# An attention and gated-MLP kernel: V tiles set once, copies placed by an estimate of two queues, 15 packed score batches, one x block loaded by itself

## Chip, cores, metric

The kernel runs on one core of one Trainium2 chip. The metric is device time in microseconds (us), lower is better. The granted clock is the share of TensorE's full clock that the trace records. Engines are named as in the profile: PE is TensorE, PEld its weight loads, DVE is VectorE, ACT is ScalarE, POOL is GpSimd, SP issues most DMAs.

## The reference

One transformer block on x of 2048 x 512, bf16. After a layer norm, two branches are added to x: attention with 32 heads of 16, causal with a window of 256 keys, and a gated linear MLP of width 1792.

```python
def _A_ref(x, wqkv, wo):                       # H = 32, Dh = 16, W = 256
    q, k, v = ...                              # of x @ wqkv
    scores = jnp.einsum("bhqd,bhkd->bhqk", q, k) * (Dh ** -0.5)
    mask = (idx[:, None] - idx[None, :] >= 0) & (idx[:, None] - idx[None, :] < W)
    p = _softmax(jnp.where(mask[None, None], scores, -1e9), axis=-1)
    return ...einsum("bhqk,bhkd->bhqd", p, v)... @ wo
def _B_ref(x, w_gate, w_up, w_down):
    h = (x @ w_gate) * (x @ w_up)
    return h @ w_down
xn = _layernorm(x)
return x + _A_ref(xn, ...) + _B_ref(xn, ...)
```

## The kernel before

The 2048 rows go in four chunks T of 512. PE's stream is laid out by hand: every few dense 512-column matmuls (gate, up, down, projections: the "fillers") a batch of small score matmuls is put in. ScalarE takes the exp of each batch, VectorE masks its diagonal, GpSimd masks its far edge with up to 4 affine selects. The row sums of the softmax come from columns of ones that stand in the V tile beside the values.

```python
# tiles: four PSUM banks "M" for dense results, the two value sums included;
# four banks for the one score tile S
self.ps_m = pool("ps_m", 4, space=bass.MemoryType.PSUM)
# ... setup
for lo, hi in ((0, 1), (1, 4)):                # x block 0, then blocks 1 to 3
    nc.sync.dma_start(out=self.x[:, lo:hi, :], in_=xv[:, lo:hi, :])
for _ in range(38):                            # warm-up
    nc.tensor.matmul(wps[:], lhsT=ident[:], rhs=ident[:], start=True, stop=True)
# ...
def new_chunk(self, T):                        # a filler of no cost, once a chunk
    self.V[T] = self.chunk3.tile([128, VW], BF16, tag="V", name=f"V{T}")
    # ... Q, K, Ko, VS
    nc.gpsimd.memset(self.heads(self.V[T])[:, :, :, 16:18], 1.0)
    nc.gpsimd.memset(self.V[T][:, VW - 16:], 0.0)
    nc.gpsimd.memset(self.VS[T][:, SW - 16:], 0.0)
def proj_v(self, t, ks=range(4)):              # ... four matmuls into a bank M, then
    nc.scalar.activation(out=self.heads(self.V[T])[:, b]..., in_=ps..., func=ACT.Copy)
def gate(self, T, f, ks):                      # likewise for K and Q
    if self.act_free:                          # 11 units or more after the last batch
        nc.scalar.activation(out=self.gsb[:], in_=ps[:], func=ACT.Copy)
    else:
        nc.vector.tensor_copy(out=self.gsb[:], in_=ps[:])
# first chunk: for b in 0..3: normalize block b on VectorE, statistics of block b + 2;
# then transposes and V projections of the four blocks, then K and Q
```

The softmax here doesn't subtract the row's maximum and nothing guards it: scores larger than these inputs give would overflow.

Of the kernel before, what the change touches and what calls it, by code (L numbers as in the profile page):

```python
# [18 lines left out]
FIRST = (((5, 5, 7), (0, 0, 4)), ((3, 3, 5), (1, 1, 5)),  # L19
         ((3, 6, 7), (7, 7, 7), (2, 2, 6)), ((4, 4, 7), (6, 6, 7)))  # L20
LATER = (((-2, 0, 2), (0, 0, 4)), ((5, 5, 7), (1, 1, 5)), ((-3, 0, 1), (7, 7, 7), (3, 3, 7)),
         ((-4, 0, 0), (6, 6, 7), (2, 2, 6)), ((-1, 0, 3), (4, 4, 7)))
ACT_FREE = 11


class Kernel:
# [26 lines left out]
    def setup(self):  # L53
# [11 lines left out]
        for lo, hi in ((0, 1), (1, 4)):  # L65
            nc.sync.dma_start(out=self.x[:, lo:hi, :], in_=xv[:, lo:hi, :])
# [41 lines left out]
        self.strips, self.at = {}, {}  # L108

    def new_chunk(self, T):  # L110

        self.Q[T] = self.chunk2.tile([128, 4, 512], BF16, tag="Q", name=f"Q{T}")
        self.K[T] = self.chunk3.tile([128, 4, 512], BF16, tag="K", name=f"K{T}")
        self.Ko[T] = self.chunk3.tile([128, 4, 512], BF16, tag="Ko", name=f"Ko{T}")
        self.V[T] = self.chunk3.tile([128, VW], BF16, tag="V", name=f"V{T}")
        self.VS[T] = self.chunk3.tile([128, SW], BF16, tag="VS", name=f"VS{T}")
        nc = self.nc
        nc.gpsimd.memset(self.heads(self.V[T])[:, :, :, 16:18], 1.0)
        nc.gpsimd.memset(self.V[T][:, VW - 16:], 0.0)
        nc.gpsimd.memset(self.VS[T][:, SW - 16:], 0.0)  # L120
# [21 lines left out]
    def norm_stats(self, t, n=4):  # L142

        nc = self.nc
        if t % n == 0:
            self.mv = self.small.tile([128, n, 2], F32, tag="mv", name="mv")
        st = self.small.tile([128, 6], F32, tag="st")
        nc.vector.bn_stats(out=st[:], in_=self.x[:, t, :])  # L148
        nc.vector.bn_aggr(out=self.mv[:, t % n, :], in_=st[:])
        self.stats[t] = [self.mv, t % n, None]  # L150
# [13 lines left out]
    def norm_apply(self, t):  # L164
        nc = self.nc
        mv, j, rs = self.stats.pop(t)
        xn = self.xpool.tile([128, 512], BF16, tag="xn", name="xn")
        nc.vector.tensor_scalar(out=xn[:], in0=self.x[:, t, :], scalar1=mv[:, j, 0:1],  # L168
                                scalar2=rs[:, j:j + 1], op0=ALU.subtract, op1=ALU.mult)
        self.xns[t] = xn  # L170
# [24 lines left out]
    def proj_v(self, t, ks=range(4)):  # L195
        nc = self.nc
        T, b = divmod(t, 4)
        ps = self.bank(ks, "vp")
        for k in ks:
            nc.tensor.matmul(ps[:], lhsT=self.xnT[T][:, b, k, :],  # L200
                             rhs=self.Wqkv[:, k, 1024:1536], start=(k == 0), stop=(k == 3))
        if 3 not in ks:
            return
        nc.scalar.activation(out=self.heads(self.V[T])[:, b].rearrange("p (r g) d -> p r g d", r=2)[:, :, :, 0:16],
                             in_=ps.rearrange("p (g r d) -> p r g d", g=16, r=2), func=ACT.Copy)

    def proj_qk(self, T, c, is_k, ks=range(4), on_act=False):
        nc = self.nc
        lo = 512 * is_k + 128 * c
        ps = self.bank(ks, "qkp")  # L210
        for k in ks:
            nc.tensor.matmul(ps[:], lhsT=self.Wqkv[:, k, lo:lo + 128], rhs=self.xnT[T][:, :, k, :],  # L212
                             start=(k == 0), stop=(k == 3))
        if 3 not in ks:
            return
        if is_k:
            if self.act_free:
                nc.scalar.activation(out=self.K[T][:, c, :], in_=ps[:], func=ACT.Copy)
            else:
                nc.vector.tensor_copy(out=self.K[T][:, c, :], in_=ps[:])  # L220
            nc.vector.tensor_scalar(out=self.Ko[T][:, c, :], in0=self.K[T][:, c, :],
                                    scalar1=self.odd[:, 0:1], scalar2=None, op0=ALU.mult)
        elif on_act or self.act_free:
            nc.scalar.activation(out=self.Q[T][:, c, :], in_=ps[:], func=ACT.Copy)
        else:
            nc.vector.tensor_copy(out=self.Q[T][:, c, :], in_=ps[:])

    def first_chunk(self):

        self.new_chunk(0)  # L230
        for b in range(2):
            self.norm_stats(b, 1)
            self.norm_scale(b, 1)
        for b in (0, 1, 2, 3):
            self.norm_apply(b)
            if b < 2:
                self.norm_stats(b + 2, 1)
                self.norm_scale(b + 2, 1)
        self.norm_transpose(0, False)
        for b in range(4):  # L240
            if b < 3:
                self.norm_transpose(b + 1, False)
            self.proj_v(b)
        self.proj_qk(0, 0, 1)
        self.proj_qk(0, 0, 0, on_act=True)
        self.swap_halves(0, self.nc.scalar)
        self.proj_qk(0, 1, 1)


    def scores(self, T, c, pieces):  # L250

        nc = self.nc
        S = self.s_tiles.tile([128, 4, 512], F32, tag="S", name="S")
        col = 0
        for m, q0, q1 in pieces:
            U, j = divmod(8 * T + m, 8)
            keys, q, n = slice(64 * j, 64 * j + 64), 64 * q0, 64 * (q1 - q0 + 1)
            for par in range(2):
                for e in range(4):
                    rows = slice(32 * e, 32 * e + 16 + 16 * par)  # L260
                    nc.tensor.matmul(S[64 * par:64 * par + 64, e, col:col + n],  # L261
                                     lhsT=(self.Ko if par else self.K)[U][rows, c, keys],
                                     rhs=self.Q[T][rows, c, q:q + n],
                                     start=True, stop=True, tile_position=(32 * e, 64 * par),
                                     skip_group_check=True)
            col += n
        P = self.ppool.tile([128, 4, 512], BF16, tag="P", name="P")
        nc.scalar.activation(out=P[:, :, 0:col], in_=S[:, :, 0:col], func=ACT.Exp, scale=0.25)  # L268
        self.strips[(T, c, pieces)] = P
# [4 lines left out]
    def places(self, pieces, far):  # L274

        out, at = [], 0
        for m, q0, q1 in pieces:
            out += [at + 64 * (q - q0) for q in range(q0, q1 + 1) if q == m + far]
            at += 64 * (q1 - q0 + 1)
        return out  # L280

    def mask_diag(self, T, c, pieces):

        P = self.strips[(T, c, pieces)]
        places = [at // 64 for at in self.places(pieces, 0)]
        step = places[1] - places[0] if len(places) == 2 else 1
        v = P.rearrange("p e (b x) -> p e b x", x=64)[:, :, places[0]:places[-1] + 1:step, :]
        n = len(places)
        self.nc.vector.tensor_tensor(out=v, in0=v, op=ALU.min,  # L289
                                     in1=self.diag.unsqueeze(1).unsqueeze(1).to_broadcast([128, 4, n, 64]))  # L290

    def values(self, T, c, accs=None):
# [5 lines left out]
        todo = []  # L298
        for pieces in LATER if T else FIRST:
            P, col = self.strips.pop((T, c, pieces)), 0  # L300
            for m, q0, q1 in pieces:
                todo.append((P, col, m, 64 * q0, 64 * (q1 - q0 + 1)))
                col += 64 * (q1 - q0 + 1)
# [17 lines left out]
        for par in range(2):  # L321
            nc.vector.transpose(out=at[:, par].rearrange("p b r -> p (b r)"), in_=accs[par][:])  # L322
        self.at[(T, c)] = at

    def divide(self, T, c):
# [5 lines left out]
        if c == 0:  # L331
# [3 lines left out]
                                in1=rz.unsqueeze(3).to_broadcast([128, 2, 16, 16]), op=ALU.mult)  # L335
        nc.vector.transpose(out=self.OT[T][:, c, :], in_=on.rearrange("p b r d -> p (b r d)"))


    def gate(self, T, f, ks):
# [10 lines left out]
        if self.act_free:  # L350
            nc.scalar.activation(out=self.gsb[:], in_=ps[:], func=ACT.Copy)  # L351
        else:
            nc.vector.tensor_copy(out=self.gsb[:], in_=ps[:])  # L353

    def up(self, T, f, ks):
# [7 lines left out]
        nc.vector.tensor_tensor(out=self.hT[T][:, f, :], in0=ps[:], in1=self.gsb[:], op=ALU.mult)  # L363

# [28 lines left out]
    def store(self, T, b, part=0, on_act=False):  # L393
# [7 lines left out]
        else:  # L401
            nc.vector.tensor_tensor(out=y, in0=ps, in1=self.x[:, t, c0:c1], op=ALU.add)
        (nc.scalar if on_act else nc.sync).dma_start(out=self.out_d[128 * t:128 * t + 128, c0:c1], in_=y)


    def fillers(self):
# [73 lines left out]
        for b in range(4):  # L480
# [3 lines left out]
            if b in (1, 3):  # L484
                add(1, lambda b=b: self.add_x(T, b, 0 if b == 1 else 1))
        return [(*o, None, None)[:4] for o in out]

    def run(self):
        self.xns, self.stats, self.sums = {}, {}, {}
        self.act_free = False  # L490
# [5 lines left out]
        for T in range(NCH):  # L496
            for c in range(4):
                self.first[T, c] = len(steps)
                for pieces in LATER if T else FIRST:
                    self.last[T, c] = len(steps)  # L500
                    steps.append((T, c, pieces))
        due = {g: key for key, g in self.last.items()}
        SCORES, VALUES = 1.85, 5.5
# [3 lines left out]
        spent, n, scored = 0, 0, 0  # L507
        valued, ready = -1, -1

        def fill(upto, group):  # L510
            nonlocal spent, n
            while n < len(work):
# [6 lines left out]
                self.act_free = spent + cost - scored >= ACT_FREE  # L519
                f()  # L520
                spent += cost
                n += 1

        def values(g):
            nonlocal spent
            if g not in due:
                return False
            self.values(*due[g])
            spent += VALUES
# [7 lines left out]
        for g, s in enumerate(steps):  # L537
            fill(-1, g)
            valued = ready
            self.scores(*s)  # L540
            scored = spent
            spent += SCORES
# [21 lines left out]
        for b in range(3):  # L564
            self.wo(T, b, (3,))
            self.store(T, b, on_act=(b == 1))
# [42 lines left out]
```

## Time and profile before

| | before |
|---|---|
| median of 3 runs | 269.21 us (269.17 to 269.22) |
| profiled span | 267.5 us |
| PE, DVE, ACT, POOL busy | 97%, 68%, 64%, 43% |

From the page of the kernel before: the span, the busy times of part 1, and part 4, the chain of work that ended last, followed back from the end and summed by engine and by line.

```profile
span 267.5 us, 8861 instructions
...
PE 258.4 (97%) x3860; PEld 119.1 (45%) x3882; DVE 181.7 (68%) x352; ACT 170.6 (64%) x132; POOL 113.8 (43%) x281
...
PE 88%; DVE 7%; issue 1%; DMA 1%; ACT 1%; SPq 0%; POOL 0%; DVEq 0%; POOLq 0%
PE up L359 17%; PE gp L345 17%; PE psd L378 16%; PE qkp L212 11%; PE S L261 9%; PE acc L316 6%; PE psd L384 5%; PE vp L200 4%; PE L L378 2%; DMA x<-in_A_x_dram 1%; DVE hT L363 1%; DVE st L148 1%; DVE at L322 1%; DVE gsb L353 1%; DVE xn L168 1%
```

PE carries the chain. The 7% of DVE in it are about 19 us, of which some 13 lie in one stretch that comes below.

The opening, from the timeline of the kernel before (columns: start us, duration us, engine, line, operation, out<-in, shapes, count, and in brackets the engine's idle time before it and what ended it):

```profile
4.80 0.70 DVE L148 BATCH_NORM_STATS2 st<-x 128x6 f32<-128x512 bf16 x1 [0.84 <-DMA x<-in_A_x_dram]
...
5.63 0.38 DVE L168 TENSOR_SCALAR xn<-x,mv,rs 128x512 bf16<-128x512 bf16 x1
...
9.14 0.41 DVE L168 TENSOR_SCALAR xn<-x,mv,rs 128x512 bf16<-128x512 bf16 x1 [0.77 <-POOL rs L160]
...
11.74 0.59 PE L212 MATMUL qkp<-xnT,Wqkv 128*128 128x512 bf16 x2
```

The statistics of block 1 wait for the load of blocks 1 to 3. Everything to the last normalize at 9.14 follows from that, and the dense stream of PE (first qkp matmul at 11.74) from the last normalize.

A place that I read too quickly, from the same timeline, with DVE's rows left in:

```profile
36.51 0.68 DVE L353 CAST gsb<-gp 128x512 bf16<-128x512 f32 x1
36.56 0.60 PE L359 MATMUL up<-xnT,Wu 128*128 128x512 bf16 x2
...
37.24 1.02 PE L345 MATMUL gp<-xnT,Wg 128*128 128x512 bf16 x4
...
42.47 0.69 DVE L363 TENSOR_TENSOR hT<-up,gsb 128x512 bf16<-128x512 f32 x1
...
42.89 0.26 PE L316 MATMUL acc<-P,VS 64*32 64x192 bf16 x4
...
43.22 0.33 PE L316 MATMUL acc<-P,V 64*32 64x192 bf16 x8
```

Two up matmuls start at 36.56 and 226 ns later, so the gate matmul should start 216 ns after that, at 37.01 (six qkp matmuls from 11.74 take 1.46 us, the last of them drawn 0.38 long: 1.08 / 5 = 0.216). It starts at 37.24, just after VectorE's gate copy ends at 37.19, which by the program frees the bank that it read. The value matmuls likewise break off until VectorE's product ends at 43.16: this group of 72 takes 1.26 us up to the next dense matmul, the groups before and after it 0.96. No missing record can be the reason at the gate matmul: the page of the kernel before counts 224 gate and 224 up matmuls, which is all of them (4 chunks x 14 column blocks x 4). The busy time hides such stalls: a matmul is drawn 380 ns long while the next can start 216 ns after it, so a stall of 0.23 us leaves 0.07 us of idle in the picture, and no line among PE's waits. VectorE is full there, busy for 13.03 of 13.5 us.

### The profile page before, as it was taken

The numbers are of one execution on the slowest core, as the hardware profiler recorded it, in microseconds if no ns is written. First come the engines' busy times: TensorE is split into PE (matmuls) and PEld (weight loads), VectorE is DVE, ScalarE is ACT, GpSimd is POOL, SyncE is SP. The second block draws the span as 40 slices with busy tenths as digits, with TensorE's granted clock in tenths as the row PEclk, the third lists the DMA queues.
The fourth block names the chain that finished last, engine by engine and source line by source line (L and its number), as shares of the span: only waits on it lengthen the run. The fifth ranks groups of instructions, "written<-read, shape, count | busy, mean of one in ns | idle before, by whom it ended". The sixth has DMA issues, their size and how long they took to land.

```text
span 267.5 us, 8861 instructions
## 1 busy us (share of the span) xinstructions
PE 258.4 (97%) x3860; PEld 119.1 (45%) x3882; DVE 181.7 (68%) x352; ACT 170.6 (64%) x132; POOL 113.8 (43%) x281
## 2 busy tenths in 40 slices
PE   6899999999999999999999999999999999999994
PEld 6444434444444444444444444444444444434453
DVE  4377898958756859676674868857762575978251
ACT  2675658696556776769656676668765667665500
POOL 5215333422674533345556433545444353443500
PEclk9999999999999999999999999999999999999999
DMA  6999911120023000001014100000200010000002
GB/s 205 373 358 334 250 22 22 23 47 0 4 61 81 20 2 4 2 2 44 5 23 97 43 0 5 0 4 2 44 5 20 26 39 2 2 0 2 4 2 81
DMA packets 19336, 15.13 MB, mean 57 GB/s; under 512 B 7264, under 2 KB 19296, under 8 KB 19296
## 3 DMA queue, kind: packets, MB, share of 16 engines
q1 hardware_dynamic: 18464, 14.09, 18.1%
q8 instruction: 30, 0.49, 0.7%
q10 hardware_dynamic: 832, 0.46, 0.6%
q14 instruction: 10, 0.08, 0.1%
HBM read 9.70 MB, written 2.10 MB: 44 GB/s over the span
## 4 chain that ended last, share of the span: by engine, by line
PE 88%; DVE 7%; issue 1%; DMA 1%; ACT 1%; SPq 0%; POOL 0%; DVEq 0%; POOLq 0%
PE up L359 17%; PE gp L345 17%; PE psd L378 16%; PE qkp L212 11%; PE S L261 9%; PE acc L316 6%; PE psd L384 5%; PE vp L200 4%; PE L L378 2%; DMA x<-in_A_x_dram 1%; DVE hT L363 1%; DVE st L148 1%; DVE at L322 1%; DVE gsb L353 1%; DVE xn L168 1%
## 5 line engine op out<-in xcount | busy, mean ns | idle before, releaser
L268 ACT ACTIVATE P<-S 128x2048 bf16<-128x2048 f32 x76 | 141.0, 1855 | 57.4 <-PE S L261 49.9
L137 POOL TENSOR_SCALAR_AFFINE_SELECT P<-P 64x256 bf16<-64x256 bf16 x224 | 97.3, 434 | 128.9 <-ACT P L268 118.2
L345 PE MATMUL gp<-xnT,Wg 128*128 128x512 bf16 x224 | 60.0, 380 | 0.1
L359 PE MATMUL up<-xnT,Wu 128*128 128x512 bf16 x224 | 59.6, 380 | 0.0
L378 PE MATMUL psd<-Wd,hT 128*128 128x512 bf16 (+1 forms) x198 | 48.7, 368 | 1.4 <-issue 1.3
L363 DVE TENSOR_TENSOR hT<-up,gsb 128x512 bf16<-128x512 f32 x56 | 38.4, 686 | 16.0 <-PE up L359 14.4
L289 DVE TENSOR_TENSOR P<-P,diag 128x512 bf16<-128x512 bf16 (+1 forms) x76 | 30.6, 404 | 10.4 <-ACT P L268 10.4
L322 DVE STREAM_TRANSPOSE at<-acc 128x512 f32<-128x512 f32 x30 | 19.7, 695 | 19.7 <-PE acc L316 19.7
L378 PEld LDWEIGHTS <-hT 128*128 128x128 bf16 x238 | 21.6, 98 | 25.3 <-issue 2.6
L359 PEld LDWEIGHTS <-Wu 128*128 128x128 bf16 x224 | 20.4, 98 | 25.3 <-issue 2.5
L345 PEld LDWEIGHTS <-Wg 128*128 128x128 bf16 x224 | 20.3, 98 | 25.5 <-issue 2.7
L261 PE MATMUL S<-Q,K 16*64 16x320 bf16 (+1 forms) x720 | 31.2, 260 | 0.4
L261 PE MATMUL S<-Q,Ko 32*64 32x320 bf16 (+1 forms) x720 | 31.1, 260 | 0.0
L212 PE MATMUL qkp<-xnT,Wqkv 128*128 128x512 bf16 x128 | 30.0, 380 | 0.0
L261 PEld LDWEIGHTS <-K 16*64 16x64 bf16 x720 | 12.2, 103 | 32.2 <-issue 32.2
L353 DVE CAST gsb<-gp 128x512 bf16<-128x512 f32 x36 | 24.5, 681 | 2.6 <-PE gp L345 1.3
L351 ACT ACTIVATE gsb<-gp 128x512 bf16<-128x512 f32 x20 | 11.9, 597 | 11.8 <-PE gp L345 11.1
L316 PE MATMUL acc<-P,VS 64*32 64x320 bf16 (+4 forms) x672 | 18.9, 254 | 0.0
L316 PE MATMUL acc<-P,V 64*32 64x320 bf16 (+4 forms) x672 | 18.4, 254 | 0.1
L212 PEld LDWEIGHTS <-Wqkv 128*128 128x128 bf16 x128 | 11.7, 98 | 14.5 <-issue 1.4
L384 PE MATMUL psd<-Wo,OT 128*128 128x512 bf16 (+1 forms) x55 | 15.5, 368 | 0.6 <-issue 0.6
L316 PEld LDWEIGHTS <-V 64*32 64x32 bf16 x720 | 14.5, 90 | 2.8 <-issue 2.4
(55 smaller groups left out, 194.1 us busy)
## 6 DMA issues: line engine op xcount, KB each, us to landing
Wg<-in_B_w_gate_dram SPq DMA_DIRECT2D x2, 896.0 KB, 10.4
Wu<-in_B_w_up_dram SPq DMA_DIRECT2D x2, 896.0 KB, 13.0
Wd<-in_B_w_down_dram SPq DMA_DIRECT2D x1, 1792.0 KB, 17.3
out_dram<-y SPq DMA_DIRECT2D x14, 128.0 KB, 1.8
Wqkv<-in_A_wqkv_dram SPq DMA_DIRECT2D x3, 512.0 KB, 6.4
x<-in_A_x_dram SPq DMA_DIRECT2D x1, 1024.0 KB, 10.9
VS<-V SPq DMA_DIRECT2D x6, 144.0 KB, 2.6
x<-in_A_x_dram SPq DMA_DIRECT2D x1, 512.0 KB, 11.4
```

Source lines behind the costliest of these rows:

```text
L137: nc.gpsimd.affine_select(out=v, in_=v, pattern=pattern + [[1 if diag else -1, 64]], compare_op=ALU.is_ge if diag else ALU.is_gt, fill=0.0 ...
L212: nc.tensor.matmul(ps[:], lhsT=self.Wqkv[:, k, lo:lo + 128], rhs=self.xnT[T][:, :, k, :], start=(k == 0), stop=(k == 3))
L261: nc.tensor.matmul(S[64 * par:64 * par + 64, e, col:col + n], lhsT=(self.Ko if par else self.K)[U][rows, c, keys], rhs=self.Q[T][rows, c, ...
L268: nc.scalar.activation(out=P[:, :, 0:col], in_=S[:, :, 0:col], func=ACT.Exp, scale=0.25)
L289: self.nc.vector.tensor_tensor(out=v, in0=v, op=ALU.min, in1=self.diag.unsqueeze(1).unsqueeze(1).to_broadcast([128, 4, n, 64]))
L316: nc.tensor.matmul(accs[par][32 * e:32 * e + 32, q:q + n], lhsT=v, rhs=P[rows, e, col:col + n], start=(i == 0), stop=(i == len(todo) - 1), ...
L345: nc.tensor.matmul(ps[:], lhsT=self.Wg[:, k, 128 * f:128 * f + 128], rhs=self.xnT[T][:, :, k, :], start=(k == 0), stop=(k == 3))
L353: nc.vector.tensor_copy(out=self.gsb[:], in_=ps[:])
L359: nc.tensor.matmul(ps[:], lhsT=self.Wu[:, k, 128 * f:128 * f + 128], rhs=self.xnT[T][:, :, k, :], start=(k == 0), stop=(k == 3))
L363: nc.vector.tensor_tensor(out=self.hT[T][:, f, :], in0=ps[:], in1=self.gsb[:], op=ALU.mult)
L378: nc.tensor.matmul(ps, lhsT=self.hT[T][:, f, 128 * b:128 * b + 128], rhs=self.Wd[:, f, c0:c1], start=(f == 0), stop=False)
L384: self.nc.tensor.matmul(ps, lhsT=self.OT[T][:, c, 128 * b:128 * b + 128], rhs=self.Wo[:, c, c0:c1], start=False, stop=(c == 3))
```

## The change

Its intent: load x block 1 alone so that the opening starts earlier; keep three V tiles for good and set their ones once; give each copy to ScalarE or VectorE by an estimate of when each queue will be free; pack the score batches of chunk 0 fully, 15 instead of 16; drop one of two matmuls that add x through an identity. Two pacing constants, what the layout of PE's stream reckons for a score batch and for a group of value matmuls, move from 1.85 and 5.5 to 1.9 and 6.0. Cut to its core:

```diff
-        for lo, hi in ((0, 1), (1, 4)):
+        for lo, hi in ((0, 1), (1, 2), (2, 4)):
...
-        self.V[T] = self.chunk3.tile([128, VW], BF16, tag="V", name=f"V{T}")   # and VS, three memsets
+        self.V[T], self.VS[T] = self.stock[T % 3]
+    def new_values(self):            # once in setup, twice at the end of the opening
+        V = self.const.tile([128, VW], BF16, name=f"V{len(self.stock)}")
+        ...                          # the same three memsets
...
+    def book(self, engine, took, ready=0):
+        self.free[engine] = max(self.free[engine], self.now, ready) + took
+    def copy(self, out, in_, engine=None):
+        if engine is None:
+            engine = min(COPY, key=lambda e: max(self.free[e], self.now) + COPY[e])
+        self.book(engine, COPY[engine])
+        ...                          # on ScalarE or VectorE
-        nc.scalar.activation(out=...V..., in_=ps..., func=ACT.Copy)
+        self.copy(...V..., ps..., engine)
-        if self.act_free: ...        # gate, K and Q likewise
+        self.copy(self.gsb[:], ps[:])
...
-FIRST = (..., ((4, 4, 7), (6, 6, 7)))          # fourth batch of a column: 6 of 8 blocks
+REST = (((0, *SIX), (1, *SIX), (0, *FOUR)), ((1, *FOUR), (2, *FOUR)), ((2, *SIX), (3, *SIX), (3, *FOUR)))
...
-            if b in (1, 3):
-                add(1, lambda b=b: self.add_x(T, b, 0 if b == 1 else 1))
+        add(1, lambda: self.add_x(T, 3, 1))
```

More of the change, by code (lines that the diff above doesn't have):

```diff
@@ L18 @@
 SW = 4 * 16 * 18 + 16
-FIRST = (((5, 5, 7), (0, 0, 4)), ((3, 3, 5), (1, 1, 5)),
-         ((3, 6, 7), (7, 7, 7), (2, 2, 6)), ((4, 4, 7), (6, 6, 7)))
+SHARED = ((5, 5, 7), (0, 0, 4)), ((3, 3, 5), (1, 1, 5)), ((3, 6, 7), (7, 7, 7), (2, 2, 6))
+FOUR, SIX = (4, 4, 7), (6, 6, 7)
 LATER = (((-2, 0, 2), (0, 0, 4)), ((5, 5, 7), (1, 1, 5)), ((-3, 0, 1), (7, 7, 7), (3, 3, 7)),
          ((-4, 0, 0), (6, 6, 7), (2, 2, 6)), ((-1, 0, 3), (4, 4, 7)))
-ACT_FREE = 11
+REST = (((0, *SIX), (1, *SIX), (0, *FOUR)), ((1, *FOUR), (2, *FOUR)), ((2, *SIX), (3, *SIX), (3, *FOUR)))
+SCORES, VALUES = 1.9, 6.0
+COPY = dict(act=2.8, dve=3.2)
+EXP, MASK, HALF, SUMS, DIVIDE, TURN, STATS = 8.7, 1.9, 1.7, 4.2, 8.2, 6.1, 4.2
 class Kernel:
@@ L107, in setup @@
         self.K, self.Ko, self.V, self.VS = {}, {}, {}, {}
-        self.strips, self.at = {}, {}
+        self.strips, self.parts, self.at = {}, {}, {}
+        self.stock = []
+        self.new_values()
     def new_chunk(self, T):
@@ L114, in new_chunk @@
         self.Ko[T] = self.chunk3.tile([128, 4, 512], BF16, tag="Ko", name=f"Ko{T}")
-        self.V[T] = self.chunk3.tile([128, VW], BF16, tag="V", name=f"V{T}")
-        self.VS[T] = self.chunk3.tile([128, SW], BF16, tag="VS", name=f"VS{T}")
+        self.V[T], self.VS[T] = self.stock[T % 3]
+    def new_values(self):
         nc = self.nc
-        nc.gpsimd.memset(self.heads(self.V[T])[:, :, :, 16:18], 1.0)
-        nc.gpsimd.memset(self.V[T][:, VW - 16:], 0.0)
-        nc.gpsimd.memset(self.VS[T][:, SW - 16:], 0.0)
+        V = self.const.tile([128, VW], BF16, name=f"V{len(self.stock)}")
+        VS = self.const.tile([128, SW], BF16, name=f"VS{len(self.stock)}")
+        nc.gpsimd.memset(self.heads(V)[:, :, :, 16:18], 1.0)
+        nc.gpsimd.memset(V[:, VW - 16:], 0.0)
+        nc.gpsimd.memset(VS[:, SW - 16:], 0.0)
+        self.stock.append((V, VS))
     def heads(self, V):
@@ L149, in norm_stats @@
         nc.vector.bn_aggr(out=self.mv[:, t % n, :], in_=st[:])
+        self.book("dve", STATS)
         self.stats[t] = [self.mv, t % n, None]
@@ L169, in norm_apply @@
                                 scalar2=rs[:, j:j + 1], op0=ALU.subtract, op1=ALU.mult)
+        self.book("dve", MASK)
         self.xns[t] = xn
@@ L193, in bank, with proj_v @@
         return self.cur
-    def proj_v(self, t, ks=range(4)):
+    def book(self, engine, took, ready=0):
+        self.free[engine] = max(self.free[engine], self.now, ready) + took
+    def copy(self, out, in_, engine=None):
+        nc = self.nc
+        if engine is None:
+            engine = min(COPY, key=lambda e: max(self.free[e], self.now) + COPY[e])
+        self.book(engine, COPY[engine])
+        if engine == "act":
+            nc.scalar.activation(out=out, in_=in_, func=ACT.Copy)
+        else:
+            nc.vector.tensor_copy(out=out, in_=in_)
+    def proj_v(self, t, ks=range(4), engine=None):
         nc = self.nc
@@ L203, in proj_v, with proj_qk @@
             return
-        nc.scalar.activation(out=self.heads(self.V[T])[:, b].rearrange("p (r g) d -> p r g d", r=2)[:, :, :, 0:16],
-                             in_=ps.rearrange("p (g r d) -> p r g d", g=16, r=2), func=ACT.Copy)
-    def proj_qk(self, T, c, is_k, ks=range(4), on_act=False):
+        self.copy(self.heads(self.V[T])[:, b].rearrange("p (r g) d -> p r g d", r=2)[:, :, :, 0:16],
+                  ps.rearrange("p (g r d) -> p r g d", g=16, r=2), engine)
+    def proj_qk(self, T, c, is_k, ks=range(4), engine=None):
         nc = self.nc
@@ L215, in proj_qk @@
             return
+        self.copy((self.K if is_k else self.Q)[T][:, c, :], ps[:], engine)
         if is_k:
-            if self.act_free:
-                nc.scalar.activation(out=self.K[T][:, c, :], in_=ps[:], func=ACT.Copy)
-            else:
-                nc.vector.tensor_copy(out=self.K[T][:, c, :], in_=ps[:])
             nc.vector.tensor_scalar(out=self.Ko[T][:, c, :], in0=self.K[T][:, c, :],
                                     scalar1=self.odd[:, 0:1], scalar2=None, op0=ALU.mult)
-        elif on_act or self.act_free:
-            nc.scalar.activation(out=self.Q[T][:, c, :], in_=ps[:], func=ACT.Copy)
-        else:
-            nc.vector.tensor_copy(out=self.Q[T][:, c, :], in_=ps[:])
+            self.book("dve", HALF)
     def first_chunk(self):
@@ L242, in first_chunk, with batches, scores @@
                 self.norm_transpose(b + 1, False)
-            self.proj_v(b)
-        self.proj_qk(0, 0, 1)
-        self.proj_qk(0, 0, 0, on_act=True)
+            self.proj_v(b, engine="act")
+        self.proj_qk(0, 0, 1, engine="dve")
+        self.proj_qk(0, 0, 0, engine="act")
         self.swap_halves(0, self.nc.scalar)
-        self.proj_qk(0, 1, 1)
-    def scores(self, T, c, pieces):
+        for _ in range(2):
+            self.new_values()
+        self.proj_qk(0, 1, 1, engine="dve")
+    def batches(self, T):
+        out = []
+        for c in range(4):
+            out += [tuple((c, *p) for p in pieces) for pieces in (LATER if T else SHARED)]
+            if T == 0 and c < 3:
+                out.append(REST[c])
+        return out
+    def scores(self, T, pieces):
         nc = self.nc
         S = self.s_tiles.tile([128, 4, 512], F32, tag="S", name="S")
+        P = self.ppool.tile([128, 4, 512], BF16, tag="P", name="P")
         col = 0
-        for m, q0, q1 in pieces:
+        for c, m, q0, q1 in pieces:
             U, j = divmod(8 * T + m, 8)
@@ L265, in scores @@
                                      skip_group_check=True)
+            self.parts.setdefault((T, c), []).append((P, col, m, q, n))
             col += n
-        P = self.ppool.tile([128, 4, 512], BF16, tag="P", name="P")
         nc.scalar.activation(out=P[:, :, 0:col], in_=S[:, :, 0:col], func=ACT.Exp, scale=0.25)
-        self.strips[(T, c, pieces)] = P
+        self.book("act", EXP)
+        self.masked = self.free["act"]
+        self.strips[(T, pieces)] = P
         for at in self.places(pieces, 4):
@@ L276, in places @@
         out, at = [], 0
-        for m, q0, q1 in pieces:
+        for _, m, q0, q1 in pieces:
             out += [at + 64 * (q - q0) for q in range(q0, q1 + 1) if q == m + far]
@@ L280, in places, with mask_diag @@
         return out
-    def mask_diag(self, T, c, pieces):
-        P = self.strips[(T, c, pieces)]
+    def mask_diag(self, T, pieces):
+        P = self.strips.pop((T, pieces))
         places = [at // 64 for at in self.places(pieces, 0)]
-        step = places[1] - places[0] if len(places) == 2 else 1
+        n = len(places)
+        step = places[1] - places[0] if n > 1 else 1
+        assert places == list(range(places[0], places[-1] + 1, step))
         v = P.rearrange("p e (b x) -> p e b x", x=64)[:, :, places[0]:places[-1] + 1:step, :]
-        n = len(places)
         self.nc.vector.tensor_tensor(out=v, in0=v, op=ALU.min,
                                      in1=self.diag.unsqueeze(1).unsqueeze(1).to_broadcast([128, 4, n, 64]))
+        self.book("dve", MASK, self.masked)
     def values(self, T, c, accs=None):
@@ L297, in values @@
             accs = [self.ps_m.tile([128, 512], F32, tag="M", name="acc") for _ in range(2)]
-        todo = []
-        for pieces in LATER if T else FIRST:
-            P, col = self.strips.pop((T, c, pieces)), 0
-            for m, q0, q1 in pieces:
-                todo.append((P, col, m, 64 * q0, 64 * (q1 - q0 + 1)))
-                col += 64 * (q1 - q0 + 1)
+        todo = self.parts.pop((T, c))
         for i, (P, col, m, q, n) in enumerate(todo):
@@ L322, in values @@
             nc.vector.transpose(out=at[:, par].rearrange("p b r -> p (b r)"), in_=accs[par][:])
+        self.book("dve", TURN)
         self.at[(T, c)] = at
@@ L335, in divide @@
                                 in1=rz.unsqueeze(3).to_broadcast([128, 2, 16, 16]), op=ALU.mult)
+        self.book("dve", DIVIDE)
         nc.vector.transpose(out=self.OT[T][:, c, :], in_=on.rearrange("p b r d -> p (b r d)"))
@@ L349, in gate @@
         self.gsb = self.work.tile([128, 512], BF16, tag="gsb", name="gsb")
-        if self.act_free:
-            nc.scalar.activation(out=self.gsb[:], in_=ps[:], func=ACT.Copy)
-        else:
-            nc.vector.tensor_copy(out=self.gsb[:], in_=ps[:])
+        self.copy(self.gsb[:], ps[:])
     def up(self, T, f, ks):
@@ L363, in up @@
         nc.vector.tensor_tensor(out=self.hT[T][:, f, :], in0=ps[:], in1=self.gsb[:], op=ALU.mult)
+        self.book("dve", COPY["dve"])
     def down(self, T, b, lo, hi):
@@ L402, in store @@
             nc.vector.tensor_tensor(out=y, in0=ps, in1=self.x[:, t, c0:c1], op=ALU.add)
+            self.book("dve", COPY["dve"])
         (nc.scalar if on_act else nc.sync).dma_start(out=self.out_d[128 * t:128 * t + 128, c0:c1], in_=y)
@@ L489, in run @@
         self.xns, self.stats, self.sums = {}, {}, {}
-        self.act_free = False
+        self.now, self.free = 0, dict(act=0, dve=0)
         self.setup()
@@ L496, in run @@
         for T in range(NCH):
-            for c in range(4):
-                self.first[T, c] = len(steps)
-                for pieces in LATER if T else FIRST:
+            for pieces in self.batches(T):
+                for c, *_ in pieces:
+                    self.first.setdefault((T, c), len(steps))
                     self.last[T, c] = len(steps)
-                    steps.append((T, c, pieces))
+                steps.append((T, pieces))
         due = {g: key for key, g in self.last.items()}
-        SCORES, VALUES = 1.85, 5.5
         self.beside = {}
@@ L506, in run @@
         total = sum(w[0] for w in work) - RESERVE + SCORES * len(steps) + VALUES * (len(due) - 1)
-        spent, n, scored = 0, 0, 0
+        spent, n = 0, 0
+        self.free = dict(act=0, dve=0)
         valued, ready = -1, -1
@@ L518, in fill @@
                     break
-                self.act_free = spent + cost - scored >= ACT_FREE
+                spent += cost
+                self.now = spent
                 f()
-                spent += cost
                 n += 1
@@ L527, in values @@
                 return False
+            spent += VALUES
+            self.now = spent
             self.values(*due[g])
-            spent += VALUES
             return True
@@ L539, in run @@
             valued = ready
+            spent += SCORES
+            self.now = spent
             self.scores(*s)
-            scored = spent
-            spent += SCORES
             upto = total * (g + 1) / len(steps)
@@ L565, in run @@
             self.wo(T, b, (3,))
-            self.store(T, b, on_act=(b == 1))
+            self.store(T, b)
         fill(10 ** 9, -1)
```

## The prediction

Two clauses that no run of this case shows are cut from it and marked; no term of its sum of 1.1 us is among them.

> **What bounds the kernel now.** TensorE's instruction stream. The page gives PE 258.4 of 267.5 us busy; [...]I read start times in the timeline. Twelve 512-column qkp matmuls take 2.76 us with a modelled last one of 0.38: (2.76-0.38)/11 = 216 ns from start to start[...]. From 11 us to the last Wo matmul (263.8 us) I find no longer gap but the fixed ones around small matmuls (309 ns before each score batch) and a few of twice 216 ns, missing records. The chain of waits agrees: PE 88%. VectorE (68%) and ScalarE (64%) wait FOR PE. Only an earlier start, fewer PE instructions or a shorter tail save time.
>
> **What the change does, costed.**
> 1. x block 1 by itself. At the start: DMA of x blocks 1 to 3 (issued 1.25, landed 4.78), three rounds of statistics and normalize on VectorE, 1.19 us each, last normalize at 9.14, then transposes and V projections. Block 0's normalize queues behind block 1's statistics. A 128 KB load took 2.0 us from issue to landing (block 0), so block 1 should land near 3.3 and its statistics start at 3.97, after the small add that ends at 3.95, instead of 4.80. Blocks 2 and 3, issued 0.45 us later, should land at 5.0 to 5.2, about when needed. Warm-up matmuls hold the first transpose to 5.4 (was 6.07); later rounds rule. The V third of Wqkv lands at about 6.7 instead of 6.22, needed at 6.7. Estimate: 0.6 to 0.85 us, all critical.
> 2. 15 batches instead of 16 in chunk 0: same matmuls, one entry into a batch less. Four batches of a column cost about 1.73 us of PE, 6.9 for four columns, against 15 x 0.45 = 6.8: 0.1 to 0.2 us. ScalarE: four exps of 1.45 us go, three of 1.88 come: 0.15 us, off the path.
> 3. One of two x-through-identity matmuls goes: 0.22 us of PE. Its store moves to VectorE (0.69 us).
> 4. Copies by estimate. By the instructions' order ScalarE's copies go from 47 to 60, VectorE's from 57 to 44. PE's order hardly changes. Before, PE never waits for a copy: this can gain nothing, only add stalls.
> 5. Fixed V tiles: three groups of GpSimd memsets (0.33 us the largest) leave mid-run. Nothing (GpSimd 43% busy).
>
> Sum: 0.75 + 0.15 + 0.22 = 1.1 us. Predicted 268.1 us, 80% range 267.3 to 269.0. Chances: faster by over 2% 0.01, within 0.975, slower 0.015.
>
> **What would show each step.** Timeline: block 1's statistics near 4.0; last normalize near 8.4; first qkp matmul 0.6 to 0.85 us before 11.74. Seventy-five exps; one identity matmul less. Dense matmuls still 216 ns apart everywhere, PE waiting for no copy. ScalarE busy about +7 us, VectorE about -9 us.
>
> **What would make it wrong.** Score batches share one PSUM tile: a batch can start when the exp before has ended. That leaves 0.63 us in the median, 0.05 and 0.15 at the tightest places. A 0.6 us copy on ScalarE between two exps (now also pairs and a triple) can delay an exp and then PE, a few tenths each. And blocks 2 and 3 of x, or the V weights, landing later than estimated would eat step 1.

## More of the kernel before

The windows view for 30 to 43.5 us (length, then busy us and count of PE, PEld, DVE, ACT and POOL, granted clock, DMA share and rate):

```profile
30.00:43.50 13.50, 13.37 (x233) 6.00 (x240) 13.03 (x26) 8.69 (x7) 5.49 (x13) 1.00 0.32 60
```

And one line of the view of waits of the kernel before (who waited for whom: us in total, times, longest), ScalarE's V copy waiting for a GpSimd memset:

```profile
ACT V L204 <- POOL V L118: 1.4, 1, 1.4
```

The same place in the timeline of the kernel before. The exp behind that copy ends late, and the score batch after the qkp matmuls waits for it:

```profile
118.28 0.60 ACT L204 ACTIVATE V<-vp 128x512 bf16<-128x512 f32 x1 [1.38 <-POOL V L118]
118.78 1.87 ACT L268 ACTIVATE P<-S 128x2048 bf16<-128x2048 f32 x1
...
120.03 0.59 PE L212 MATMUL qkp<-xnT,Wqkv 128*128 128x512 bf16 x2
...
120.70 0.22 PE L261 MATMUL S<-Q,K 16*64 16x64 bf16 x4
```

## The result

| | before | after |
|---|---|---|
| median of 4 runs each | 269.19 us (268.81 to 269.22) | 267.37 us (267.35 to 267.42) |
| ratio, 95% interval | | 0.9936, 0.9919 to 0.9953 |
| profiled span | 267.5 us | 265.6 us |
| first qkp matmul | 11.74 us | 11.12 us |
| stream: first qkp to start of last matmul | 252.02 us | 250.89 us |
| last matmul start to end of span | 3.75 us | 3.57 us |

A ratio is the mean time of one kernel's fast runs over that of the other's of the same rounds, so it is not quite the ratio of the medians quoted. The gain is 1.82 us. The time, 267.37 us, is inside the predicted range of 267.3 to 269.0, but only 0.07 us from its low end; the point was 268.1. By the traces the span lost 0.62 us in the opening, 1.13 us in the stream, and 0.18 us in the tail. The tail is chance: it lies between 3.46 and 3.76 us over all profiles, with the same instructions.

Some of the 1.82 us is chance too. The executions of before under 270 us in the four later calls have medians of 268.8 to 269.0 us, where three of the four here took 269.2. In the profile of before the load of x blocks 1 to 3 landed at 4.78 us, later than in any other profile that has it. The version a_oldcopies, whose stream is as long as that of after, is 1.49 us faster than before in its own call. After itself was not run again, so about 1.5 us is what the change is worth as far as this record tells.

The page of the kernel after, same lines:

```profile
span 265.6 us, 8876 instructions
...
PE 257.5 (97%) x3860; PEld 119.0 (45%) x3881; DVE 176.1 (66%) x339; ACT 176.4 (66%) x143; POOL 114.6 (43%) x278
...
PE 94%; DVE 2%; issue 1%; DMA 1%; POOL 0%
```

PE's busy share is 97% as before. What moved is the chain: DVE fell from 7% of it to 2%. The opening from its timeline:

```profile
3.93 0.69 DVE L158 BATCH_NORM_STATS2 st<-x 128x6 f32<-128x512 bf16 x1
...
4.75 0.38 DVE L179 TENSOR_SCALAR xn<-x,mv,rs 128x512 bf16<-128x512 bf16 x1
...
8.18 0.33 POOL L127 MEMSET V<- 128x256 bf16 x1
...
8.27 0.83 DVE L179 TENSOR_SCALAR xn<-x,mv,rs 128x512 bf16<-128x512 bf16 x1 [0.77 <-POOL rs L171]
...
8.53 0.33 POOL L127 MEMSET V<- 128x256 bf16 x1
...
11.12 2.75 PE L239 MATMUL qkp<-xnT,Wqkv 128*128 128x512 bf16 x12
```

Block 1's statistics start at 3.93 (predicted 3.97) and the last normalize 0.87 us earlier than before, but it takes 0.83 instead of 0.41 us: the memsets of the second and third V tile now stand beside it (a_memset_early, below, tests this). The windows view of the kernel after, 30 to 43.5 us:

```profile
30.00:43.50 13.50, 13.50 (x276) 6.33 (x276) 11.64 (x23) 10.66 (x10) 5.03 (x12) 1.00 0.32 62
```

PE has no idle time left there, VectorE has lost 1.4 us of work. Where the kernel before stood still after two up matmuls, the timeline of the kernel after, at the like place, has the gate matmuls 0.44 us behind the first up matmul, two slots:

```profile
36.06 0.60 PE L390 MATMUL up<-xnT,Wu 128*128 128x512 bf16 x2
...
36.50 1.03 PE L379 MATMUL gp<-xnT,Wg 128*128 128x512 bf16 x4
```

In start times, the kernel before has three stalls in its stream: 0.23 us at 37.2, 0.30 us at 43.2, and 0.14 us at 120.7 (a score batch 447 instead of 309 ns after the dense matmul ahead of it, waiting for an exp). The kernel after has none. That is 0.67 us that the prediction did not have. No line of the waits of the kernel after has ScalarE waiting for a memset. Of the forecasts of busy time, ScalarE +7 us and VectorE -9 us, +5.8 and -5.6 came.

### The profile page after: what moved, and what is told of

It is laid out like the page before. It is cut to its first block, busy times and chain, and to the rows that moved or that the text cites. A ratio compares the mean times of both kernels' runs of the same rounds, so it can differ in the third digit from the quotient of the medians.

```text
span 265.6 us, 8876 instructions
## 1 busy us (share of the span) xinstructions
PE 257.5 (97%) x3860; PEld 119.0 (45%) x3881; DVE 176.1 (66%) x339; ACT 176.4 (66%) x143; POOL 114.6 (43%) x278
## 4 chain that ended last, share of the span: by engine, by line
PE 94%; DVE 2%; issue 1%; DMA 1%; POOL 0%
PE up L390 19%; PE gp L379 19%; PE psd L410 16%; PE qkp L239 11%; PE S L294 10%; PE acc L348 7%; PE psd L416 5%; PE vp L227 5%; PE L L410 2%; DVE st L158 1%; DMA x<-in_A_x_dram 1%; PE L L416 1%; DVE xn L179 1%; PE L L348 0%; DVE mv L159 0%
## 5 line engine op out<-in xcount | busy, mean ns | idle before, releaser
L147 POOL TENSOR_SCALAR_AFFINE_SELECT P<-P 64x256 bf16<-64x256 bf16 x224 | 98.6, 440 | 128.9 <-ACT P L301 117.9
L379 PE MATMUL gp<-xnT,Wg 128*128 128x512 bf16 x224 | 58.9, 380 | 0.0
L325 DVE TENSOR_TENSOR P<-P,diag 128x512 bf16<-128x512 bf16 (+1 forms) x75 | 29.9, 399 | 9.8 <-ACT P L301 9.8
L294 PE MATMUL S<-Q,K 16*64 16x320 bf16 (+4 forms) x720 | 30.9, 260 | 0.1
L294 PE MATMUL S<-Q,Ko 32*64 32x320 bf16 (+4 forms) x720 | 31.0, 260 | 0.0
L218 ACT ACTIVATE gsb<-gp 128x512 bf16<-128x512 f32 x34 | 20.0, 596 | 15.5 <-PE gp L379 13.5
L220 DVE CAST gsb<-gp 128x512 bf16<-128x512 f32 x22 | 15.2, 691 | 3.4 <-PE gp L379 2.0
L416 PE MATMUL psd<-Wo,OT 128*128 128x512 bf16 (+1 forms) x59 | 16.2, 369 | 0.2 <-issue 0.2
```

The source lines that it names most:

```text
L147: nc.gpsimd.affine_select(out=v, in_=v, pattern=pattern + [[1 if diag else -1, 64]], compare_op=ALU.is_ge if diag else ALU.is_gt, fill=0.0 ...
L218: nc.scalar.activation(out=out, in_=in_, func=ACT.Copy)
L294: nc.tensor.matmul(S[64 * par:64 * par + 64, e, col:col + n], lhsT=(self.Ko if par else self.K)[U][rows, c, keys], rhs=self.Q[T][rows, c, ...
L325: self.nc.vector.tensor_tensor(out=v, in0=v, op=ALU.min, in1=self.diag.unsqueeze(1).unsqueeze(1).to_broadcast([128, 4, n, 64]))
L379: nc.tensor.matmul(ps[:], lhsT=self.Wg[:, k, 128 * f:128 * f + 128], rhs=self.xnT[T][:, :, k, :], start=(k == 0), stop=(k == 3))
L416: self.nc.tensor.matmul(ps, lhsT=self.OT[T][:, c, 128 * b:128 * b + 128], rhs=self.Wo[:, c, c0:c1], start=False, stop=(c == 3))
```

## The experiments

All twelve were correct. "Stream" is as in the table above, from the start times in the trace. It leaves out the opening, whose length depends on when loads land (the load of x blocks 1 to 3 landed at 4.33 to 4.78 us in the profiles that have it). Times are medians of six runs. The fourth column is the median of before in the same call without its executions above 270 us, for a reason that comes under "The slow executions"; the other columns leave nothing out. First qkp and stream come from the one profiled execution.

| run | edit | median us | before | first qkp us | stream us |
|---|---|---|---|---|---|
| a_oldcopies | after, old rule for copies | 267.33 | 268.82 | 11.06 | 250.89 |
| b_copies | before, copies by estimate | 269.35 (three near 268.5, three near 270.2) | 268.82 | 11.30 | 251.54 |
| b_xsplit | before, x block 1 alone | 268.36 | 268.82 | 11.07 | 251.96 |
| a_memset_early | after, memsets moved earlier | 267.12 | 268.82 | 10.81 | 250.89 |
| b_15 | before, 15 batches | 271.95 | 268.78 | 11.38 | 255.05 |
| b_pacing | before, new pacing | 270.96 | 268.78 | 13.07 | 254.20 |
| a_nosplit | after, blocks 1 to 3 together | 267.74 | 268.78 | 11.62 | 250.90 |
| b_noident | before, one identity matmul less | 270.76 | 268.78 | 11.30 | 253.97 |
| b_fixedV | before, fixed V tiles | 268.53 | 268.96 | 11.51 | 251.91 |
| b_15_fixedV | 15 batches and fixed V tiles | 268.01 | 268.96 | 11.36 | 251.24 |
| a_chunkmemset | after, V set in every chunk | 270.85 | 268.96 | 10.95 | 254.29 |
| b_20warm | before, 20 warm-up matmuls | 270.60 | 268.88 | 13.65 | 252.03 |

### Copies: from both ends

Theory A: the estimate removed the stalls. Rival B: batches and pacing did.

```diff
 a_oldcopies, on after
-            engine = min(COPY, key=lambda e: max(self.free[e], self.now) + COPY[e])
+            engine = "act" if self.act_free else "dve"     # proj_v: always "act"
```

> The kernel after with the old rule for copies (V always ScalarE, K, Q and gate on ScalarE only 11 units after a score batch), all else as after. Theory A (the extra 0.7 us over the prediction is three TensorE stalls of before, 0.23 + 0.31 + 0.14 us, made by copies queued on the wrong engine): stalls of 0.3 to 0.7 us in all come back, ratio to before about 0.9955 (268.0 us). Rival B (the 15 packed batches and the new pacing removed them): no stall comes back, ratio stays at 0.9935 (267.4 us).

Measured: 267.33 us, stream 250.89 us to the digit as in after, no stall came back. These are the numbers of rival B.

```diff
 b_copies, on before
+    book() and copy() of the change; every copy through copy(); bookings as in the change
```

> The kernel before with only the copies given by the estimate; batches, pacing, x blocks, V tiles and the identity matmuls as before. Theory A: the gaps of 446, 315 and 447 ns in TensorE's stream go, first qkp matmul still at 11.74; ratio 0.9975 (268.5 us). Rival B: the gaps stay or others come, ratio 1.000.

Measured: two of the three gaps go and the stream is 0.48 us shorter, close to what A wants (a value group at 145 us is 0.05 us longer); the third, at a score batch, stays (450 ns at 119.7 us). Taking the three runs near 268.5, the gain is 0.34 us. So both ends speak against a single cause: the copies alone remove the pair of stalls, and the rest of the change removes them without the copies. The windows view fits this, 30 to 43.5 us, first b_copies, then a_oldcopies:

```profile
30.00:43.50 13.50, 13.50 (x270) 6.44 (x263) 11.41 (x23) 10.82 (x10) 5.29 (x12) 1.00 0.38 58
```

```profile
30.00:43.50 13.50, 13.50 (x277) 6.29 (x268) 12.44 (x25) 9.82 (x8) 4.95 (x12) 1.00 0.50 58
```

VectorE was busy for 13.03 of these 13.5 us before; 11.41 and 12.44 leave it some room. With 15 batches the distance between batches grows, and the old rule ("ScalarE takes a copy 11 units after a batch") then catches more gates: of the 14 gate copies of chunk 0 ScalarE took 5 before, 7 in a_oldcopies, 10 in b_copies and after.

### x block 1, and the memsets beside the normalize

```diff
 b_xsplit, on before (a_nosplit: the reverse, on after)
-        for lo, hi in ((0, 1), (1, 4)):
+        for lo, hi in ((0, 1), (1, 2), (2, 4)):
```

> The kernel before with only x block 1 loaded by itself. Theory C (in the kernel after, the V memsets that now stand in the opening collide with the last normalize, 0.83 instead of 0.41 us): without them here the last normalize takes 0.41 us and the first qkp matmul is 0.85 us earlier than 11.74; ratio 0.9970. Rival D (the opening is limited elsewhere): first qkp matmul 0.62 us earlier as in the kernel after, ratio 0.9977.

Measured: 268.36 us, 0.46 us faster. First qkp matmul at 11.07, 0.67 us earlier than in the profile of before: between C and D. Block 1 landed only at 4.10 here (3.27 in after), so the start of the stream does not tell them apart. The last normalize does: it takes 0.41 us here, as in all eleven profiles without memsets beside it, and 0.83 in the three with them (after, a_oldcopies, a_nosplit).

> The kernel after without the split of x block 1. Theory C: first qkp matmul 0.3 to 0.65 us later than 11.12 (it depends on when blocks 1 to 3 land, which was 4.33 and 4.78 in two profiles), stream still 250.9 us, ratio to before 0.995. Theory F (the runs at about 270.3 us that before and the run with only the copies show in a part of their executions come from the 384 KB load landing late): some executions are 1.5 us longer. Rival to F: none is, as in the four other versions with the split.

Measured: first qkp at 11.62, 0.50 us later than in after; stream unchanged. So the split is worth about half a microsecond, all in the opening. None of its six executions was 1.5 us longer, which speaks against F, but weakly: of 44 executions of before 10 were.

```diff
 a_memset_early, on after: all three new_values() in setup, in POOL's idle time at 3 to 4 us
         self.stock = []
-        self.new_values()
+        for _ in range(3):
+            self.new_values()
```

> The kernel after with the memsets of the second and third V tile moved from the last normalize to GpSimd's idle time at 3 to 4 us. Theory C: last normalize 0.41 us again, first qkp matmul at about 10.87 instead of 11.12, ratio to before 0.9926 (267.1 us). Rival D: the normalize stays at 0.83 us or the stream starts no earlier, ratio 0.9935.

Measured: 267.12 us against 267.33 for a_oldcopies in the same rounds, whose stream is equal; first qkp at 10.81. Its last normalize, from the timeline of a_memset_early:

```profile
8.19 0.41 DVE L180 TENSOR_SCALAR xn<-x,mv,rs 128x512 bf16<-128x512 bf16 x1 [0.77 <-POOL rs L172]
```

C holds: with no memset beside it, it takes 0.41 us again, against 0.83 with them. By what means the memsets slow the normalize, and which of the two waits, the traces do not show. By its median this is the fastest version; after itself (267.37) was not run in this call.

### Single parts that cost two to three microseconds

```diff
 b_15, on before: SHARED, REST, batches() and parts of the change, nothing else
```

> The kernel before with only the 15 packed batches in chunk 0 (old rule for copies, old pacing constants). Its ScalarE takes 6 gate copies in chunk 0, 5 in before, 7 in the last run with the old rule on top of the kernel after, 10 in after. From first qkp to last matmul start, before took 252.02 us. Theory A' (each of copies by estimate and 15 batches removes the two stalls near 37 and 43 us by itself): 252.02 - 0.24 for the batch - about 0.5 = 251.3 us, no gap of 446 or 315 ns. Rival E (it took the batches and the new pacing together): 251.8 us with stalls left. The third stall (447 ns near 120.7 us, a batch behind a late exp) is open to both.

```diff
 b_pacing, on before
-        SCORES, VALUES = 1.85, 5.5
+        SCORES, VALUES = 1.9, 6.0
```

> The kernel before with only the pacing constants 1.9 and 6.0. Theory A': the two stalls near 37 and 43 us stay, as VectorE has the same copies there; stream 251.9 to 252.1 us, ratio 1.000. Rival E: they go, stream 251.5.

```diff
 b_noident, on before
-            if b in (1, 3): ...      # add_x for block 1 goes; its store to VectorE
```

> The kernel before without the identity matmul of the second to last x block, its store on VectorE. Stream 252.02 - 0.22 = 251.8 us, ratio 0.999. Theory F: some executions are 1.5 us longer, as the load is not split.

None of the expectations came true: 271.95, 270.96 and 270.76 us. (In one point A' did: with the new pacing alone the stalls near 37 and 43 us stay, 445 ns and a value group of 1.25 us.) Three parts that look neutral or good each made the kernel about 2 to 3 us slower. The waits of b_15 that before does not have, or has smaller:

```profile
ACT V L205 <- POOL V L119: 5.0, 2, 2.6
...
PE S L272 <- ACT P L279: 1.7, 2, 0.9
...
PE qkp L213 <- ACT V L205: 1.4, 2, 1.2
```

The place itself, from the timeline of b_noident:

```profile
180.77 1.88 ACT L268 ACTIVATE P<-S 128x2048 bf16<-128x2048 f32 x1 [0.72 <-PE S L261]
...
182.71 2.09 POOL L137 TENSOR_SCALAR_AFFINE_SELECT P<-P 64x256 bf16<-64x256 bf16 x4 [2.59 <-ACT P L268]
...
184.86 0.33 POOL L118 MEMSET V<- 128x256 bf16 x1
...
185.22 1.57 ACT L204 ACTIVATE V<-vp 128x512 bf16<-128x512 f32 x3 [2.57 <-POOL V L118]
185.87 1.89 PE L212 MATMUL qkp<-xnT,Wqkv 128*128 128x512 bf16 x8 [1.20 <-ACT V L204]
186.66 1.90 ACT L268 ACTIVATE P<-S 128x2048 bf16<-128x2048 f32 x1
...
188.62 0.30 PE L261 MATMUL S<-Q,K 16*64 16x256 bf16 x4 [0.86 <-ACT P L268]
```

Read it downwards. An exp ends at 182.65. GpSimd's four selects wait for it and take 2.09 us. The V memset of the next chunk stands behind them in GpSimd's queue. ScalarE's next instruction is a V copy that waits for the memset, 2.57 us; PE meanwhile fills the banks with V projections and stops (1.20 us). The next exp stands behind the V copies, so the next score batch waits too (0.86 us). By start times the two stops are longer, 1.37 and 0.93 us, 2.30 in all: with the identity matmul's 0.22 us and the stall at 120.7, which this run does not have, taken off, this gives a stream of 253.96 us against 253.97 measured. The trace shows that ScalarE did not take the exp ahead of the copies: it stood idle for 2.57 us, up to 185.22, although the scores of the next batch lay ready from 183.7, and their exp started at 186.66, after three V copies.

Whether this happened in a profile went with the program as built. Counted in the order of its instructions, the length of the unbroken run of selects ahead of the V memsets of chunk 2 and of chunk 3:

```
before, b_copies, b_xsplit   38   38
b_noident, b_pacing          38   42    one stall, at 186 and 188 us
b_15                         42   42    two stalls, at 121 to 124 and 187 to 192 us
after with memsets per chunk 42   42
```

With 38 the memset stands ahead of that batch's four selects, with 42 behind them. Moving the fillers by one batch, for whatever reason, puts it on the wrong side. Theory G, which the next expectations state, says this is all of it.

### Fixed V tiles, alone and as the rescue

```diff
 b_fixedV, on before; b_15_fixedV, on b_15
-        self.V[T] = self.chunk3.tile(...)      # and three memsets in every chunk
+        self.V[T], self.VS[T] = self.stock[T % 3]      # set in setup, at 3 to 4 us
```

> The kernel before with only the three fixed V tiles, their memsets in GpSimd's idle time at 3 to 4 us. Theory G (V memsets stand in GpSimd's queue behind the affine selects of a score batch; ScalarE's V copies wait for the memset, the next exp waits behind them; where 42 selects instead of 38 come before the memset this costs TensorE about 2.1 us): before has 38 twice, so only its ScalarE wait of 1.4 us near 117 us and the 447 ns gap near 120.7 us go, 0.14 us, and no execution at about 270.3 us appears; the gaps near 37 and 43 us stay. Median 268.5 to 268.8 us, stream 251.9. Rival H (the 2.1 us come from elsewhere): slow executions stay.

Measured: 268.53 us (268.49 to 268.73), stream 251.91 us. The gap at 120.7 is gone, those at 37 and 43 us are there (443 and 311 ns). The median is 0.43 us below before in the same call, but the stream gives only 0.11 of it; what gave the rest is not shown.

> The 15 batches of the last call again (271.95 us) with the three fixed V tiles. Theory G: its two stalls near 121 to 124 and 187 to 192 us go, 4.2 us in all; the stream is 251.8 less the batch's 0.24 and what goes of the stalls near 37 and 43 us, so 251.2 to 251.6 us; total about 268.2 us. Rival H: it stays above 270 us.

Measured: stream 251.24 us and median 268.01, from 271.95 without the tiles: 3.9 us, and in the stream 3.8. Of the two stalls of 0.53 us, 0.13 us is left (346 ns at 36.9 us), so the batches remove most of the pair without the estimate. Two of six executions were at 269.6 and 270.0 though; G had nothing on those.

```diff
 a_chunkmemset, on after
-        self.V[T], self.VS[T] = self.stock[T % 3]
+        self.V[T] = self.chunk3.tile(...)      # and three memsets in every chunk, as before
```

> The kernel after with the V tiles rotating and set in every chunk as before, nothing else undone. By the order of its GpSimd instructions both later memsets stand behind 42 selects. Theory G: ScalarE (or VectorE) waits over 2 us for the memset at chunks 2 and 3, TensorE stalls twice, 3 to 4.5 us in all, total 270 to 271.8 us. The prediction on record (fixed tiles are worth nothing): 267.4 us.

Measured: 270.85 us. The stream is 254.29 us, 3.40 more than after. From its waits and its timeline we read the same chain, with both copying engines held. From the timeline of a_chunkmemset:

```profile
184.46 0.33 POOL L121 MEMSET V<- 128x256 bf16 x1
...
184.82 1.09 ACT L211 ACTIVATE V<-vp 128x512 bf16<-128x512 f32 x2 [2.39 <-POOL V L121]
184.82 1.29 DVE L213 CAST V<-vp 128x512 bf16<-128x512 f32 x2 [1.65 <-POOL V L121]
...
187.73 0.30 PE L285 MATMUL S<-Q,K 16*64 16x256 bf16 x4 [1.24 <-ACT P L292]
```

So without the fixed tiles the change would have been a loss of about 1.9 us against before; the part that I called worth nothing decides its sign.

### The slow executions

Of the 44 executions of before ten took 270.2 to 270.9 us, the others 268.6 to 269.3, all counted as fast. The profile of b_pacing happened to fall into such an execution (272.55 us, its others mostly 270.7 to 271.0). PE's rows in it, from the timeline:

```profile
7.26 1.91 PE L200 MATMUL vp<-Wqkv,xnT 128*128 128x512 bf16 x4
...
9.40 1.62 PE L200 MATMUL vp<-Wqkv,xnT 128*128 128x512 bf16 x4
```

Four V projections take 1.91 us there, 426 ns from start to start, where b_noident in an ordinary execution has:

```profile
7.04 1.03 PE L200 MATMUL vp<-Wqkv,xnT 128*128 128x512 bf16 x4
```

In the trace's record of the granted clock, full speed begins at 10.60 us in that execution, at 4.15 to 6.80 in the twelve other profiles before the last run. The trace shows the clock and the spacing; what made full speed begin so late in that execution it does not show. To test whether a late full speed costs this much, the warm-up was cut, on the guess that fewer of its matmuls delay full speed:

```diff
 b_20warm, on before
-        for _ in range(38):
+        for _ in range(20):
```

> The kernel before with 20 warm-up matmuls instead of 38[...]. Theory J (the executions of before at 270.3 to 270.9 us are those in which the granted clock is still half when the V projections start, as in the profile of the run with only the pacing constants: full clock from 10.6 us, V projections 426 ns apart): every execution is 1.5 to 3 us longer than the fast ones of before, V projections 426 ns apart, none near 268.8 us. Theory F (a late load of x blocks 1 to 3 makes them): the warm-up is not on the path, fast and slow executions are mixed as in before.

Measured: 269.89 to 271.13 us, no execution near 268.8, one (269.89) clearly below the expected range. From the timeline of b_20warm:

```profile
7.41 1.91 PE L200 MATMUL vp<-Wqkv,xnT 128*128 128x512 bf16 x4
```

V projections stand 426 ns apart, full speed begins at 12.17 us (5.97 in the profile of before), the first qkp matmul is at 13.65 instead of 11.74, and the stream is 252.03 us, as in before. So J's forecast came and F's did not, and in the slow profile of b_pacing the load landed as early as elsewhere, at 4.38 us. That a late clock costs this much is shown (1.72 us by the medians of b_20warm and of before in that call, 270.60 and 268.88); that it is what made the ten executions of before slow is inferred, as none of the ten was profiled. In the 28 executions of versions with x block 1 alone none was that slow; one of b_xsplit was 0.8 us longer. That the split is the reason is not shown: none of the six of a_nosplit or of b_fixedV, which load blocks 1 to 3 together, was that slow either, so this stays open.

## Why the prediction was right, and where its sum was off

The class and the range were right. The sum, 1.1 us, was short of the measured 1.82 by 0.7, and of the 1.5 of the later calls by 0.4. Two errors of opposite sign partly hid each other: 0.67 us of stalls that the prediction denied, and about 0.25 us too much for x block 1. That the range held, by 0.07 us, is in part luck. Point by point:

1. x block 1: predicted 0.75, measured 0.62 between the two profiles and 0.50 against a_nosplit. The mechanism held to 0.04 us at block 1's statistics. What I left out is that the change also puts memsets beside the last normalize: 0.42 us on VectorE, 0.21 us of time by the medians and 0.25 at the first qkp matmul (a_memset_early against a_oldcopies).
2. 15 batches: predicted 0.1 to 0.2. From start times, 16 batches with their entries take 7.00 us of PE and 15 take 6.77: 0.23. Alone, in the setting of before, it costs 3.2 us.
3. Identity matmul: 0.22 us as predicted, counted as one 216 ns slot; no run isolates it, as alone it costs 2.0 us.
4. Copies: this is the step that failed. "Before, PE never waits for a copy: this can gain nothing, only add stalls" was wrong. It rested on "I find no longer gap but the fixed ones ... and a few of twice 216 ns, missing records". Most double gaps are missing records (the page of before counts 3860 matmuls to 3882 weight loads, its view of lines 60 of the 64 V projections), but the 446 ns at 37.2 is not, and 315 and 447 ns at 43.2 and 120.7 are no multiples. I took a list of gaps for one kind because most of them were. The chain of waits said it plainly: from 29.7 to 43.2 us it runs almost only through VectorE, and DVE's 7% fell to 2%. The pair of stalls, 0.53 us, goes with the copies alone (b_copies), or without them with the new batches and pacing in fixed tiles (a_oldcopies): either suffices.
5. Fixed V tiles: "Nothing (GpSimd 43% busy)" was wrong. They removed the third stall, 0.14 us (gone in b_fixedV, whose stream is 0.11 shorter), and they are what lets steps 2 and 3 be had at all: 3.4 us in a_chunkmemset. I judged a memset by the load of its engine; its cost here came from its place in that engine's queue.

The sum then closes for the stream: 0.23 + 0.22 + 0.53 + 0.14 = 1.12 against 1.13 measured. With 0.62 of the opening and 0.18 of a tail that varies by chance, this is the 1.93 us of the span.

The risk that I named, pairs of copies delaying an exp, did not come: after has no such stall.

## What to carry to other kernels

Look at matmuls by start-to-start times, and prove for every odd gap that a record is missing before calling it so: count the records of that line against the program. A share of VectorE in the chain of a kernel bound by PE can be a stretch where VectorE sets the pace, as from 29.7 to 43.2 us here. A short instruction on an engine that is idle over half the time can cost far more than it takes when two engines wait on it in turn: in b_noident a 0.33 us memset behind 2.09 us of selects held ScalarE for 2.57 us and TensorE for 2.30 us by start times. Ask what stands ahead of it and who waits behind it, and take such one-time work out of the loop. When a layout is tuned, undoing or adding one part can move such an instruction across a batch, so test a part both alone on the old kernel and missing from the new one.
